# Attention with memory and a spectral filter on one core: a unit's scores split over two score steps, PSUM divided 3+2+3, and a new written-out order

## The chip, the core and the metric

The kernel runs on one core of a Trainium2 chip. The core has five engines with their own instruction streams: TensorE (PE, matmuls; its weight loads are listed as PEld), VectorE (DVE), ScalarE (ACT), GpSimd (POOL) and SyncE (SP, which here only issues DMAs). PE writes to PSUM, which is divided into eight banks of 512 fp32 columns; ACT and DVE read PSUM and move results to SBUF ("evict" them). The metric is the device time of one execution in microseconds, lower is better; the figure for a kernel is the median of its runs.

## The reference

The input is x, 2048 tokens of 640 features. Three things are computed and mixed: a causal attention in four segments of 512 tokens with 32 heads of 20 features, with a compressed memory carried from segment to segment; a filter in the two-dimensional Fourier domain; and a gate per token. Cut to what matters:

```python
q, k, v = heads(x @ wq), heads(x @ wk), heads(x @ wv)      # 32 heads of 20, 4 segments of 512
for s in range(4):
    p = softmax(qs @ ks.T * 20**-0.5 + causal_mask)
    a_dot = p @ vs
    a_mem = (phi(qs) @ M) / (phi(qs) @ z + 1e-6)           # phi(t) = t+1 if t > 0 else exp(t)
    outs.append(g * a_mem + (1 - g) * a_dot)               # g = sigmoid(beta), per head
    M, z = M + phi(ks).T @ vs, z + phi(ks).sum(0)
a = concat(outs) @ wo
b = irfft2(rfft2(x) * (w_r + 1j * w_i))                    # over tokens and features
gate = sigmoid((x * gate_w).sum(-1, keepdims=True))
return gate * a + (1 - gate) * b
```

## The kernel before

**How the program is made.** The class `Kern` records operations (`Sched.op`, L66): what each reads and writes, which engines can do it (`copy_alts`, L534: ACT or DVE; `either`, L549: DVE or POOL), what it should cost, and which PSUM banks it uses (`Bank`, L32). `Sched.schedule` (L117) takes a long list, `ORDER` (L594), and emits the operations in that order on each engine: an entry is twice the number of the record plus the choice of engine. So the order on every engine and the division of work between engines are written out by hand in that list. `schedule` steps through it with assumed costs only to choose physical banks and DMA semaphores, and from data dependences and bank reuse `emit` (L258) makes the semaphore waits. A queue is kept in order: an instruction that waits holds back all behind it on its engine.

**PSUM.** `POOLS` (L587) gives banks 0 to 3 to the scores (`qk`) and banks 4 to 7 to everything else (`gen`).

**Attention.** A segment has eight groups of four heads, taken in four pairs. A pair has five units (`UNITS`, L588): for each of its two groups the first 128 and the next keys' part (kind 0 and kind 1), and one unit of kind 2, that holds the small diagonal rest of both groups. So there are 80 units. `qk_unit` (L1242) writes the scores of a unit: its four heads have 20 features each and lie in four 32-row strips of the PE array, which work at the same time, each head into its own PSUM bank, so that one unit takes all four banks of `qk`. The pieces of a head are in `PIECES` (L589). Then one ACT instruction (two in the last segment for kinds 1 and 2, 92 in all) at L1278 takes the exponential of all four banks to the tile `ex`:

```python
bank = Bank(4, "qk")
for j, kc, p0, q0, o, n in self.PIECES[kind]:
    for hh in range(4): ...
self.one("act", lambda e, d=d, q=q: e.activation(self.ex.ap(*d), self.ps(bank, *q), ACT.Exp, scale=SC), n, [bank], ...)
```

The next unit's scores need the same four banks, and so wait for that instruction. POOL masks `ex` in place (`mask`, L1296, instructions on L1299), and PE multiplies with v (`pv_flipped`, L1193, for segments 0 to 2; `pv_group`, L1304, for segment 3).

**Beside it.** PE also makes the projections (`proj_tile`, L1042; for the first two groups `proj_direct`, L976, whose results `qkp` feed the first scores), v (`v_part`, L1115), the memory (`mem_read_tile`, `mem_update`) and the Fourier transforms as matrix products (`fft`, L1381). All of these use banks of `gen`, which ACT or DVE evict: qu, q, et (phi's exponential, L1087), va (L1130), Ac, Bt, Pt (L1455), Cp, eo and G (L1501), ub, ot. DVE and POOL fold the input rows (`fold`, L906, tiles xsb and xf) before the first transform, and add Pt to Yt (L1460). All this is laid between the units, so that from 13 to 226 us the units run through the whole program.

**The end.** Where the attention of a segment is done, its sums go through DRAM (u_scr, r_scr), and `finish_tile` (L1522) adds the product with wo to the filter's last step in one bank and evicts it to ot, which is stored. The last segment stays on chip (`last_transposes`, L1505; oTl) and uses wo2, loaded by one DMA (L1554) into the place of wk.

**The first DMAs.** SP issues one xsb load (ld_x), the transposing load of x's first 128 features (xT), beta, half of wk (ld_wka), then the two other xT loads. ACT issues ld_wqa. PE multiplies zeros (`warm_up`) until the first data come.

Of the kernel before, what the change touches and what calls it, by code (L numbers as in the profile page):

```python
# [44 lines left out]
class Op:  # L45
    __slots__ = ("id", "alts", "preds", "succs", "prio", "banks", "nbytes", "npred", "eng", "t0", "t1",
                 "stamp", "need_inc", "dyn", "first", "outside", "name", "dma", "key", "xfer", "lock", "mode", "emode", "hold", "width")


class Sched:  # L50
# [6 lines left out]
    FREE, PORT, LATE = 52.0, (85.0, 55.0), 500.0  # L57
# [59 lines left out]
    def schedule(self, pools, order, nsem=56):  # L117
# [32 lines left out]
        two = False  # L150
# [24 lines left out]
        def head(e):  # L175
# [18 lines left out]
            if o.dma:  # L194
                gate = window()
                if gate is not None:
                    t = max(t, gate.t1 + self.HOPS[e]["dma"])
            if e == "dve" and o.lock:
                t = max(t, free["pool"] + (20.0 if two else -self.PORT[0]))
            elif e == "pool":  # L200
                t = max(t, port - self.PORT[1])
            return t

        while len(self.order) < len(order):
# [20 lines left out]
            free[e] = o.t1 = t + occ  # L225
            if e == "dve" and o.lock:
                port = t + occ
            if e == "pool":
                two = o.lock
# [243 lines left out]
class Kern:  # L473
# [38 lines left out]
    def mms(self, items, r, w, prio, name="", extra=0.0, mode=0):  # L512
# [18 lines left out]
        op = self.Sc.op({"pe": (f, cost, self.DRAIN.get(name, 141.0))}, r=r, w=w, prio=prio, name=name, mode=mode)  # L531
        return op
# [10 lines left out]
    def one(self, eng, fn, n, r, w, prio, per=None, fix=None, name="", after=()):  # L543
# [3 lines left out]
        return self.Sc.op({eng: (fn, fix + per * n, late)}, r=r, w=w, prio=prio, name=name, after=after)  # L547
# [9 lines left out]
    def dma(self, dst, src, nbytes, r, w, prio, tr=False, name="", after=(), queue="sp"):  # L557
# [6 lines left out]
        cost, work, width = self.QUEUE[name] if name in self.QUEUE else self.QUEUE[name, nbytes]  # L564
        queues = ("sp", "act") if name in self.EARLY else (queue,)
        return self.Sc.op({e: (f, cost, 0.0) for e in queues}, r=r, w=w, prio=prio, nbytes=nbytes, name=name, after=after,
# [4 lines left out]
        "ld_W": (620.0, 450.0, 16), "ld_beta": (400.0, 120.0, 16), "ld_big": (500.0, 2900.0, 16), "ld_den": (520.0, 150.0, 16),  # L571
        "ld_fcat": (400.0, 350.0, 16), "ld_g": (500.0, 1900.0, 16), "ld_gc": (580.0, 200.0, 16), "ld_gw": (420.0, 600.0, 16),
        "ld_hm": (600.0, 850.0, 16), "ld_r": (570.0, 700.0, 16), "ld_tt": (530.0, 1650.0, 16), "ld_u": (530.0, 600.0, 16),
        "ld_wka": (520.0, 1100.0, 16), "ld_wkb": (450.0, 1500.0, 16), "ld_wqa": (500.0, 1100.0, 16), "ld_wqb": (500.0, 2200.0, 16),
        "ld_wo": (600.0, 700.0, 16), "ld_wo2": (600.0, 3000.0, 16), "ld_wv": (450.0, 3000.0, 16), "ld_x": (450.0, 830.0, 16),
        "oT": (1300.0, 750.0, 16), "pad2": (370.0, 200.0, 10), "pad": (400.0, 1250.0, 10), ("pkT", 131072): (1260.0, 600.0, 16), ("pkT", 262144): (1280.0, 1100.0, 16),
        ("st_qk", 65536): (450.0, 220.0, 16), ("st_qk", 131072): (480.0, 350.0, 16), ("st_qk", 262144): (480.0, 720.0, 16), "st_g": (430.0, 150.0, 4), "st_o": (660.0, 950.0, 8), "st_out": (560.0, 1900.0, 4),
        "st_part": (430.0, 250.0, 16), "st_r": (480.0, 200.0, 16), "st_u": (520.0, 700.0, 16), ("xT", 131072): (1240.0, 1300.0, 16), ("xT", 262144): (1500.0, 1400.0, 16),
        ("xT", 393216): (1400.0, 2600.0, 16), ("xT", 655360): (2950.0, 2100.0, 16)}
# [7 lines left out]
    POOLS = {"qk": [0, 1, 2, 3], "gen": [4, 5, 6, 7]}  # L587
# [648 lines left out]
    def exo(self, s, g):  # L1236
        return ((s * 8 + g) % self.NEX) * 5120
# [385 lines left out]
```

## Time and profile before

| | us |
|---|---|
| median of 3 runs | 242.91 (242.09 to 248.04) |
| the profiled execution | 240.85 |
| span of its profile, first to last instruction | 238.9 |
| ACT, exponentials of the scores (L1278), busy | 138.7 in 92 instructions |
| POOL, masks (L1299), busy | 122.0 in 224 |
| PE, score matmuls (L529, qkp 20*64), busy | 32.3 in 1280 |
| mean granted PE clock | 0.998 |

Busy time is given per engine. Matmuls overlap, so their rows last longer than the distance from one to the next; the same holds to a smaller degree for ACT and DVE. In the tables of waits "PE psum L529 <- ACT ex L1278" means that a matmul at L529, which writes psum, waited for the exponential at L1278, which writes ex. A line can be a helper's: nearly all matmuls are on L529. In the rows of the timeline the name behind the arrow tells what is read: `psum<-qkp` are scores, `psum<-xT,wq` projections. "xN" counts the instructions merged into a row.

### The profile page before, as it was taken

How to read it: one execution, taken by the hardware profiler on the slowest of the kernel's cores; microseconds unless marked ns; L12 is line 12 of the kernel's file. 1: busy time of each engine (PE TensorE's matmuls, PEld its weight loads, DVE VectorE, ACT ScalarE, POOL GpSimd, SP SyncE). 2: the span in 40 equal slices, each digit the busy share in tenths (PEclk: the TensorE clock that was granted, in tenths of full speed). 3: DMA queues.
4: the chain of work that ended last, by engine and by line, in shares of the span. 5: the costliest groups of instructions: out<-in, count | busy, mean ns of one | idle time of the engine just before them, and what ended most of it. 6: DMA issues, size and time to landing. Idle time of an engine off the chain costs nothing.

```text
span 238.9 us, 10255 instructions
## 1 busy us (share of the span) xinstructions
PE 227.6 (95%) x4361; PEld 140.1 (59%) x4361; DVE 196.6 (82%) x481; ACT 199.5 (83%) x241; POOL 166.7 (70%) x297
## 2 busy tenths in 40 slices
PE   7899999999999999999989999999999999899994
PEld 2575566775456566555646655455645466567794
DVE  0579998889899996898999798997988896846563
ACT  2189688898899999999999979999899988797730
POOL 8523268457969956937974999875889868678730
PEclk9999999999999999999999999999999999999999
DMA  7999849996996876483779572364766995872223
GB/s 171 277 366 233 231 125 185 264 207 149 250 227 158 153 210 178 110 241 72 237 213 261 171 226 62 103 157 144 204 205 162 244 215 83 121 107 83 59 86 111
DMA packets 58928, 42.17 MB, mean 177 GB/s; under 512 B 30020, under 2 KB 55172, under 8 KB 58884
## 3 DMA queue, kind: packets, MB, share of 16 engines
q1 hardware_dynamic: 57844, 40.96, 69.9%
q8 instruction: 34, 0.56, 1.0%
q10 hardware_dynamic: 1040, 0.57, 0.8%
q14 instruction: 10, 0.08, 0.2%
HBM read 23.32 MB, written 12.30 MB: 149 GB/s over the span
## 4 chain that ended last, share of the span: by engine, by line
PE 54%; DVE 19%; ACT 14%; DMA 7%; issue 3%; SPq 1%; DVEq 0%
PE psum L529 48%; ACT ex L1278 9%; PE psum L527 6%; DVE Pt L1455 3%; DMA r_scr<-rc 3%; ACT et L1087 2%; DMA xT<-in_A_x_dram 2%; DMA Wt<-in_B_w_i_dram 2%; DVE xsb L921 2%; DVE xf L916 2%; DVE G L1501 1%; DVE va L1130 1%; DVE q L540 1%; DMA r<-r_scr 1%; DVE oU L1542 1%
## 5 line engine op out<-in xcount | busy, mean ns | idle before, releaser
L1278 ACT ACTIVATE ex<-psum 128x2048 bf16<-128x2048 f32 (+4 forms) x92 | 138.7, 1508 | 12.2 <-PE psum L529 10.1
L1299 POOL TENSOR_SCALAR_AFFINE_SELECT ex<-ex 128x256 bf16<-128x256 bf16 (+2 forms) x224 | 122.0, 567 | 37.2 <-ACT ex L1278 33.7
L529 PE MATMUL psum<-qkp 20*64 20x64 bf16 (+5 forms) x1280 | 32.3, 270 | 2.2 <-ACT ex L1278 2.0
L529 PE MATMUL psum<-xT,wk 128*128 128x256 bf16 (+1 forms) x280 | 33.9, 273 | 0.2
L529 PE MATMUL psum<-xT,wq 128*128 128x512 bf16 (+1 forms) x135 | 30.7, 380 | 0.8 <-DMA xT<-in_A_x_dram 0.8
L529 PE MATMUL psum<-wv,xT 128*32 128x321 bf16 (+3 forms) x400 | 30.0, 301 | 0.3 <-DVE va L1130 0.3
L1455 DVE TENSOR_TENSOR Pt<-psum,Wt 128x642 bf16<-128x642 f32 x32 | 25.6, 822 | 2.2 <-PE psum L529 1.9
L529 PEld LDWEIGHTS psum<-qkp 20*64 20x64 bf16 x1280 | 13.3, 102 | 19.7 <-ACT ex L1278 15.4
L529 PEld LDWEIGHTS psum<-xT,wk 128*128 128x128 bf16 (+1 forms) x280 | 19.9, 97 | 6.5 <-DMA wk<-in_A_wk_dram 0.6
L527 PE MATMUL psum<-wo,oU 128*32 128x320 bf16 x480 | 21.9, 300 | 0.7 <-DVE oU L1550 0.5
L921 POOL TENSOR_TENSOR xsb<-xf 128x320 bf16<-128x320 bf16 (+2 forms) x12 | 9.5, 790 | 16.1 <-DVE xsb L921 12.4
L529 PEld LDWEIGHTS psum<-wv,xT 128*32 128x32 bf16 (+1 forms) x400 | 14.6, 96 | 7.5 <-issue 2.6
L1130 DVE TENSOR_TENSOR va<-psum,ebx 128x320 bf16<-128x320 f32 x32 | 15.2, 484 | 4.4 <-ACT gate L1128 2.1
L529 PE MATMUL psum<-big,Ac 128*128 128x160 bf16 (+2 forms) x96 | 18.1, 258 | 0.4 <-DVE Pt L1455 0.3
L529 PE MATMUL psum<-big,Cp 128*128 128x321 bf16 (+1 forms) x96 | 18.0, 302 | 0.2 <-DVE G L1501 0.2
L529 PE MATMUL psum<-ex,va 128*32 128x64 bf16 (+3 forms) x576 | 17.4, 257 | 0.4 <-DVE mem L1175 0.2
L1501 DVE TENSOR_TENSOR G<-eo,psum 128x320 bf16<-128x320 f32 x32 | 14.7, 483 | 3.6 <-PE psum L529 2.6
L540 DVE CAST ot<-psum 128x320 bf16<-128x320 f32 x21 | 10.1, 491 | 9.1 <-PE psum L527 5.9
L529 PE MATMUL psum<-tt,Yt 128*128 128x256 bf16 (+1 forms) x96 | 16.5, 276 | 0.5 <-DVE Yt L1460 0.2
L529 PEld LDWEIGHTS psum<-ex,va 128*32 128x32 bf16 x576 | 10.8, 96 | 9.6 <-POOL ex L1299 1.3
L1087 ACT ACTIVATE et<-qu 128x512 bf16<-128x512 bf16 x25 | 15.6, 631 | 0.2
L527 PEld LDWEIGHTS psum<-wo,oU 128*32 128x32 bf16 x480 | 11.9, 96 | 5.4 <-issue 1.4
(99 smaller groups left out, 392.7 us busy)
## 6 DMA issues: line engine op xcount, KB each, us to landing
qkp<-qk_scr SPq DMA_DIRECT2D x28, 160.0 KB
tt<-tab_tt SPq DMA_DIRECT2D x8, 512.0 KB, 4.5
qk_scr<-qu SPq DMA_DIRECT2D x12, 256.0 KB, 3.1
u_scr<-ub SPq DMA_DIRECT2D x12, 256.0 KB, 3.7
xsb<-in_A_x_dram SPq DMA_DIRECT2D x8, 320.0 KB, 6.5
oU<-u_scr SPq DMA_DIRECT2D x15, 128.0 KB, 2.9
out_dram<-ot SPq DMA_DIRECT2D x12, 160.0 KB
Wt<-in_B_w_r_dram SPq DMA_DIRECT2D x16, 80.2 KB, 2.6
```

Source lines behind the costliest of these rows:

```text
L527: h = e.matmul(dst, wt, r_, start=st, stop=sp_, **{**kw, "tile_position": (0, q), "skip_group_check": True})
L529: h = e.matmul(o_, l_, r_, start=st, stop=sp_, **kw)
L540: alts["dve"] = (lambda e: e.tensor_copy(dst(), src()), 67 + 1.04 * n, 68.0)
L916: self.either(lambda e, r=r, op=op: e.tensor_tensor(xf.ap(r * 642, [321, 2], [1, 320]), xs.ap(o, [D, 2], [1, 320]), xs.ap(o + 320, [D, 2], ...
L921: self.either(lambda e, dst=dst, src=src, d0=d0, n=n, op=op: e.tensor_tensor(xs.ap(o + dst, [D, 2], [1, n]), xf.ap(src + d0, [321, 2], [1, ...
L1087: self.one("act", lambda e: e.activation(et.ap(0, [1, L]), qsl(), ACT.Exp), L, [qb], [b("et", pi_)], late, fix=95, name="phi_exp")
L1130: self.one("dve", lambda e: e.tensor_tensor(va.ap(i * H * VW + h0 * VW, [VW, nh], [1, DH]), self.ps(bank, 0, [DH, nh], [1, DH]), self.ebx. ...
L1278: self.one("act", lambda e, d=d, q=q: e.activation(self.ex.ap(*d), self.ps(bank, *q), ACT.Exp, scale=SC), n, [bank], [self.exb(s, 2 * pr + ...
L1299: self.one("pool", lambda e: e.affine_select(self.ex.ap(e0 + d0, [1280, 4], [1, n], np_=np_), self.ex.ap(e0 + s0, [1280, 4], [1, n], np_=np_),
L1455: self.one("dve", lambda e, ri=ri, Pt=Pt, Wt=Wt, wo_=wo_, bank=bank: e.tensor_tensor(Pt.ap(ri * 322, [644, 2], [1, KD]), self.ps(bank, 0, ...
L1501: self.one("dve", lambda e, q=q, n2=n2, bank=bank, eo=eo: e.tensor_tensor(self.G.ap(n2 * D + 639 * q, [1 - 2 * q, 320]), eo.ap(q, [1, 320] ...
L1542: self.either(lambda e, c=c: e.tensor_tensor(oT.ap(c * L, [1, L]), oT.ap(c * L, [1, L]), self.r4[s].ap(0, [1, L]), ALU.mult), L, [b("r4", ...
```

## The change

1. **Scores.** `qk_unit` writes heads 0 to 2 of its unit and head 3 of the following unit in one step, interleaved piece by piece. The first step of a segment also writes its own head 3, the last step of a segment writes heads 0 to 2 alone.
2. **PSUM.** Three banks for heads 0 to 2, two for head 3 (one written while the other is read), three for everything else.
3. **Exponentials.** Each of the 92 becomes two: one over three heads and one over head 3 (`"y" + name`), with separate dependence keys ("d"). The masks and the product with v depend on both.
4. **The order list** is written anew (2,424 entries instead of 2,328), with other choices of engine for some evictions, folds and additions; SP starts with the three xT loads and ld_wka is on ACT's queue.
5. **wo2** is loaded in five DMAs, one per 128 rows, and each product waits for its own.
6. **The step through the list** in `schedule` assumes other DMA times, instruction fetches of PE, and the DVE/POOL port. One of this reaches the program: a POOL operation of the locked kind (two inputs), or the one after it, gets a dependence on the last locked DVE operation ahead of it (`o.dyn.append(ldv)`). Three small DVE constants are now of the locked kind.

The diff, cut to its core:

```diff
@@ Sched
-    FREE, PORT, LATE = 52.0, (85.0, 55.0), 500.0
+    FREE, PORT, LATE = 52.0, (85.0, 55.0), 0.0
...
             if e == "dve" and o.lock:
                 port = t + occ
+                ldv = o
             if e == "pool":
-                two = o.lock
+                if (o.lock or two) and ldv is not None:
+                    o.dyn.append(ldv)
+                two, ldv = o.lock, None
...
-    POOLS = {"qk": [0, 1, 2, 3], "gen": [4, 5, 6, 7]}
+    POOLS = {"qk": [0, 1, 2], "qy": [3, 4], "gen": [5, 6, 7]}
...
@@ attend
-                self.qk_unit(s, pr, u, parts)
+                k = pr * len(self.UNITS) + u + 1
+                self.qk_unit(s, pr, u, parts, (k // len(self.UNITS), self.UNITS[k % len(self.UNITS)]) if k < 4 * len(self.UNITS) else None)
...
+    def exk(self, s, g, keys):
+
+        return [self.exb(s, g, k + x) for k in keys for x in (("",) if k[0] == "m" else ("", "d"))]
...
-    def qk_unit(self, s, pr, u, unit):
-        self.Sc.group += 1
-        b = self.b
-        prio = self.texp(s, 2 * pr, u)
-        bank = Bank(4, "qk")
+    def qk_part(self, s, pr, unit, heads, bank):
+
+        b = self.b
         gps, kind = unit
         width = 128 if kind == 2 else 512
         items, rb = [], []
...
+        return items, rb, 256 if kind == 2 else 512
+
+    def qk_unit(self, s, pr, u, unit, after):
+        self.Sc.group += 1
+        b = self.b
+        prio = self.texp(s, 2 * pr, u)
+        gps, kind = unit
+        bank, first = Bank(3, "qk"), pr == u == 0
+        parts, banks = [self.qk_part(s, pr, unit, (0, 1, 2), bank)], [bank]
+        if first:
+            self.ahead = Bank(1, "qy")
+            parts.append(self.qk_part(s, pr, unit, (3,), self.ahead))
+            banks.append(self.ahead)
+        bank3 = self.ahead
+        cols = max(p[2] for p in parts)
+        if after is not None:
+            self.ahead = Bank(1, "qy")
+            parts.append(self.qk_part(s, *after, (3,), self.ahead))
+            banks.append(self.ahead)
+            cols = cols + parts[-1][2] if first else max(cols, parts[-1][2])
+        ths = [th for n_ in range(max(len(p[0]) for p in parts)) for p in parts if n_ < len(p[0]) for th in p[0][n_]]
+        self.mms([(th, cols / len(ths)) for th in ths], [x for p in parts for x in p[1]] + banks, [], prio - self.QK_LEAD, name="qk", mode=1)
...
-            self.one("act", lambda e, d=d, q=q: e.activation(self.ex.ap(*d), self.ps(bank, *q), ACT.Exp, scale=SC), n, [bank],
...
+            d3, q3 = (d[0], [d[1][0], 3]) + d[2:], (q[0], [512, 3]) + q[2:]
+            self.one("act", lambda e, d=d3, q=q3: e.activation(self.ex.ap(*d), self.ps(bank, *q), ACT.Exp, scale=SC), 3 * n, [bank],
+                     [self.exb(s, g, k) for g, k in keys], prio - self.QK_LEAD, name=name)
+            d1, q1 = (d[0] + 3 * d[1][0],) + d[2:], (q[0],) + q[2:]
+            self.one("act", lambda e, d=d1, q=q1: e.activation(self.ex.ap(*d), self.ps(bank3, *q), ACT.Exp, scale=SC), n, [bank3],
+                     [self.exb(s, g, k + "d") for g, k in keys], prio - self.QK_LEAD, name="y" + name)
...
-            self.dma(lambda: self.wo2.ap(0, [D, 5], [1, D]), lambda: dap(self.wo_d, 0, [D, P], [P * D, 5], [1, D]), P * 5 * D * 2,
-                     [], [b("wo2")], self.texp(3, 0) + 2.0, name="ld_wo2", after=[b("wka"), b("wkb")])
+            for c in range(5):
+                self.dma(lambda c=c: self.wo2.ap(c * D, [1, D]), lambda c=c: dap(self.wo_d, c * P * D, [D, P], [1, D]), P * D * 2,
+                         [], [b("wo2", c)], self.texp(3, 0) + 2.0, name="ld_wo2", after=[b("wka"), b("wkb")])
```

More of the change, by code (lines that the diff above doesn't have):

```diff
@@ L197, in head @@
                     t = max(t, gate.t1 + self.HOPS[e]["dma"])
+            if e == "pe":
+                n = o.count * (4 if o.mode < 0 and o.emode == 2 else 1)
+                k = (npe + n + 48) // 256
+                if k > 1:
+                    t = max(t, fetched[k] - 15.0 * max(0, k * 256 - 48 - npe))
+            if port_free:
+                return t
             if e == "dve" and o.lock:
@@ L201, in head @@
                 t = max(t, port - self.PORT[1])
+                if o.lock or two:
+                    if ldv is not None:
+                        t = max(t, ldv.t1 + self.HOPS["pool"]["dve"])
+                    elif pos["dve"] < len(queue["dve"]) and queue["dve"][pos["dve"]].lock:
+                        x = head("dve", True)
+                        if x is not None and x <= t - 50.0:
+                            t = max(t, free["pool"] + 21.0)
             return t
@@ L225, in schedule @@
             free[e] = o.t1 = t + occ
+            if e == "pe":
+                npe += o.count * (4 if o.mode < 0 and o.emode == 2 else 1)
+                while nblk < (npe + 48) // 256:
+                    nblk += 1
+                    fetched[nblk + 1] = max(sum(ring) / 16, o.t1 + 1300.0) + 1100.0
             if e == "dve" and o.lock:
                 port = t + occ
+                ldv = o
             if e == "pool":
-                two = o.lock
+                if (o.lock or two) and ldv is not None:
+                    o.dyn.append(ldv)
+                two, ldv = o.lock, None
             if o.dma:
@@ L541, in copy_alts, with one @@
         return alts
-    def one(self, eng, fn, n, r, w, prio, per=None, fix=None, name="", after=()):
+    def one(self, eng, fn, n, r, w, prio, per=None, fix=None, name="", after=(), lock=False):
         fix0, per0, late = {"act": (65, 0.833, 110.0), "dve": (67, 1.04, 68.0), "pool": (132, 0.945, 50.0)}[eng]
@@ L546, in one @@
         fix = fix0 if fix is None else fix
-        return self.Sc.op({eng: (fn, fix + per * n, late)}, r=r, w=w, prio=prio, name=name, after=after)
+        return self.Sc.op({eng: (fn, fix + per * n, late)}, r=r, w=w, prio=prio, name=name, after=after, lock=lock)
     def either(self, fn, n, r, w, prio, name="", after=()):
@@ L563, in f @@
                 return e.dma_start(d_, s_)
-        cost, work, width = self.QUEUE[name] if name in self.QUEUE else self.QUEUE[name, nbytes]
+        cost, work, width, late = self.QUEUE[name] if name in self.QUEUE else self.QUEUE[name, nbytes]
         queues = ("sp", "act") if name in self.EARLY else (queue,)
-        return self.Sc.op({e: (f, cost, 0.0) for e in queues}, r=r, w=w, prio=prio, nbytes=nbytes, name=name, after=after,
+        return self.Sc.op({e: (f, cost, late) for e in queues}, r=r, w=w, prio=prio, nbytes=nbytes, name=name, after=after,
                           dma=True, xfer=work, hold=tr and nbytes > 500000, width=width)
```

62 lines of the change are left out of this document (35 added, 27 removed), and 198 rows, old and new, of the table ORDER.

## The prediction

> **What bounds the kernel now.** First the page: busy shares, then the chain that ended last.
>
> ```profile
> PE 227.6 (95%) x4361; PEld 140.1 (59%) x4361; DVE 196.6 (82%) x481; ACT 199.5 (83%) x241; POOL 166.7 (70%) x297
> PE 54%; DVE 19%; ACT 14%; DMA 7%; issue 3%; SPq 1%; DVEq 0%
> ```
>
> PE is hardly ever idle and carries half the chain. Then the table by stretch (us; busy us of PE, PEld, DVE, ACT, POOL, each with its count; clock; DMA), which shows how close the others run in the middle:
>
> ```profile
> 100.00:120.00 20.00, 19.42 (x325) 11.23 (x324) 18.56 (x46) 19.51 (x24) 14.57 (x30) 1.00 0.63 177
> 140.00:160.00 20.00, 19.07 (x298) 10.20 (x294) 18.45 (x37) 18.80 (x21) 17.95 (x32) 1.00 0.42 115
> ```
>
> ACT is as full as PE there. Third, the timeline of one turn, ACT's rows and then PE's (start us, us):
>
> ```profile
> 163.38 1.88 ACT L1278 ACTIVATE ex<-psum 128x2048 bf16<-128x2048 f32 x1
> 165.15 0.59 ACT L538 ACTIVATE Cp<-psum 128x512 bf16<-128x512 f32 x1
> 165.75 1.03 ACT L1278 ACTIVATE ex<-psum 128x1024 bf16<-128x1024 f32 x1
> 166.67 0.59 ACT L538 ACTIVATE qu<-psum 128x512 bf16<-128x512 f32 x1
> 167.33 1.88 ACT L1278 ACTIVATE ex<-psum 128x2048 bf16<-128x2048 f32 x1
> ```
> ```profile
> 165.31 0.32 PE L529 MATMUL psum<-qkp 20*64 20x64 bf16 x24 [0.27 <-ACT ex L1278]
> 166.83 0.42 PE L529 MATMUL psum<-qkp 20*64 20x320 bf16 x16 [0.28 <-ACT ex L1278]
> ```
>
> The scores (qkp) start 0.05 us after an exponential ends (163.38 + 1.88 = 165.26, then 165.31), take 0.3 to 0.4, and the next exponential starts 0.1 later. All four score banks are one unit's, so PE and ACT take turns; ACT fills its turn off with an eviction, PE stands. A full turn is 1.88 + 0.05 + 0.42 + 0.08 = 2.43 us. Fourth, the waits (us in total, times, longest), and the timeline's first loads:
>
> ```profile
> PEld psum L529 <- ACT ex L1278: 15.4, 49, 0.6
> PE psum L529 <- ACT ex L1278: 2.0, 8, 0.3
> ```
> ```profile
> 1.25 1.21 SPq L561 DMA_TRANSPOSE xT<-in_A_x_dram  x1
> 3.60 2.63 SPq L561 DMA_TRANSPOSE xT<-in_A_x_dram  x2
> 7.86 0.40 PE L529 MATMUL psum<-xT,wq 128*32 128x512 bf16 x4 [0.83 <-DMA xT<-in_A_x_dram]
> ```
>
> The 15.4 is idle time of the weight loader, most of it under a matmul that still streams. To see PE's own loss I took the starts of successive groups of matmuls in the timeline, less the columns streamed (the 512-column rows follow each other in 0.215 us, so 0.42 ns a column) and a change of tile shape at about 0.1 us (projection to projection is 0.108 apart at the least, projection to scores 0.201). Lost in all: 16.1 us. Of it 3.0 to 3.5 before scores that wait for an exponential, 6.7 where a group waits for one of the four other banks to be evicted, 1.3 at 5.7 to 7.9 us for the two last xT loads, 4 to 5 for data, instruction issue and small rests.
>
> **The change, part by part.**
> *Scores three and one.* A unit's heads 0 to 2 now go with head 3 of the next unit. Matmuls stay 1,280, but a step lasts as long as its longer part: the diagonal units (24 matmuls, 0.32 us) now run beside a part of 0.43, so 16 x 0.11 = 1.8, and the first step of each segment writes head 3 twice, 512 more columns, 4 x 0.21 = 0.9. Together +2.6 us (2.56 before rounding), on PE's path. Against it, walking PE's queue through both order lists (a number is twice the record's number plus the choice of engine) I count 229 and 215 changes of tile shape: 14 x 0.11 = -1.5.
> The turn: three heads' exponential takes 1.45 us (the rows of 2048 and 1024 elements give 0.171 + 0.000834 x elements), after which its banks are free, and head 3's, whose scores lie ready, covers the 0.05 + 0.42 + 0.08 of the next scores. What PE regains lies between 2.0 (the waits of its matmul rows) and 15.4 (all of the loader's); I take 3.5, the loss counted above, because the rest lies under streaming matmuls. What is late next is ACT.
> *Exponentials in two parts.* 92 more instructions. A 2048 row is followed after 1.77 (163.38 to 165.15), not 1.88, so 0.11 of each overlaps the next; two parts occupy 1.34 + 0.49 = 1.83. So +0.06 each, 92 x 0.06 = 5.5 us of ACT. The order list moves evictions: ACT loses 4 of Ac, 2 each of Bt, Cp, oTl and the first qkp, and gains 3 of ub, 2 of ot, 1 of qu, at their rows less 0.11: -2.9. Net +2.6. ACT is idle 19.9 of the 213 us from 13 to 226 (sum of the table's stretches); that covers it: 0, bounds 0 and +2.6.
> The Trainium skill (ScalarE: Activation LUTs, What ACT_TABLE_LOAD costs) gives 186 ns plus 0.833 per element, successive ones overlapping by about 93. That would make the split 92 x 0.093 = 8.6 us, an estimate from that page; the trace's overlap here is 0.11, and the sum goes by the trace.
> *PSUM 3+2+3.* The general pool falls from four banks to three. I followed its 326 uses from first matmul to the end of the eviction: 797.6 us held, 432 filling, 127 waiting for the evicting engine, 238 in eviction; three to four held at any time. Three banks offer 3 x 238.9 = 717, less than is held now. The list answers that: fills interrupted by other work go from 168 to 126, those with scores inside from 64 to 30, and the columns and shape changes between a bank's first and last matmul from 374 to 273 us, so about 797.6 - 100 = 697 stay. With 0.06 us from release to reuse and use only from 6 to 235 us (3 x 229 = 687), 30 bank-us are missing, or 10 us of PE. A quarter off the 127 (the longest thing that an eviction waits behind on ACT falls from 1.77 to 1.34) closes it: 32. Bounds: -2.2 (a third off the 6.7) and +10; I take +1.5, nearer the rows that close it.
> *Start.* SP now issues the three xT loads first and wk goes to ACT's queue behind wq: the last two start at 0.78 + 1.21 = 1.99 instead of 3.60, 1.6 earlier. The first xsb load is pushed behind them by 1.21 + 2.63 = 3.8, and with it POOL's and DVE's first folds (at 5.72 and 7.69); the chain from 18 to 35 us is DVE's, though DVE is idle in most of the first 11. Beta too comes later on SP; it feeds constants that the first v evictions want near 20 us. Bounds -1.6 and +1; I take -1.2.
> *The rest of the order.* POOL gains 6 additions of Yt (0.73 against DVE's 0.39), 2 of oU, a gate table and small ones, less 2 folds: about +7.6 us in 72 of idleness, DVE +0.9 in 42. POOL's two-input operations now wait for the last such DVE operation before them; masks queue behind, and the last masks gate the product with v. POOL waits 33.7 us for exponentials, which hides it: 0, bounds -1 and +1. Of data and issue waits I take back 0.7 of some 4.5 (bounds 0 and 2).
> *Last weights.* wo2 in five loads instead of one: four more issues of 0.6, 2.4 us of SP, which waits 21.3 us for PE in all; the oT loads and output stores behind them could come late if that cover went, by up to 2.4. They sit between loads due some 20 us before use: 0.
>
> Sum: +2.6 - 1.5 - 3.5 + 1.5 - 1.2 - 0.7 = -2.8. The profiled execution took 240.85 (span 238.9), so 238.05 on its terms. It ran 2.06 under the median of the three runs, 242.91; on that footing the forecast is 240.1.
>
> **The rivals.**
> 1. *Evictions get quicker too, faster.* With shorter exponentials the bank waits fall by a third, -2.2 instead of +1.5: 240.1 - 3.7 = 236.4. For it: 127 us of waiting for the evicting engine; fewer interrupted fills. Against: a bank less.
> 2. *Three banks are too few, slower.* If the eviction waits stay as they are, the 10 us come in full: 240.1 + 8.5 = 248.6, worst from 60 to 200 us, where 3.3 to 3.6 of four banks are held. It decides once holds stay over about 690 us in all. Against: the shorter exponentials.
> The Trainium skill (TensorEngine Tiling (Array Packing), PSUM Bottleneck) says that packing speeds up TensorE but not PSUM's evacuation. This speaks for the second rival; the 6.7 us against 3.5 above agree that evictions cost more than scores do.
> 3. *ACT becomes the bound, no gain.* From 100 to 120 us ACT is idle for 0.5. If the turn was only as long as ACT's work, the 3.5 are not regained and up to the 2.6 are added: 243.6 to 246.2, about 244.5. Against: ACT's idle 19.9 us elsewhere.
>
> **How the numbers follow.** Forecast 0.43 (own range 238 to 242), rival 1 0.27, rival 3 0.17, rival 2 0.13. The range 235 to 246.5 takes in rivals 1 and 3 and leaves out most of the second. By more than 2%, about what can be told from no change here, means under 238.05 or over 247.8: faster is 0.8 of rival 1 and a fifth of the forecast, 0.31; slower is 0.7 of rival 2 and a sixth of rival 3, 0.12; the rest 0.57.
>
> **What would show it.** Right: scores start while a 512-element exponential runs, and waits of PE and its loader for ex shrink to a third; the first full run of projection matmuls starts at about 6.3; general banks are held 690 us or less. Wrong: longer PE waits for ub, Bt, Cp, Pt, va (second rival), or ACT without gaps and PE's unchanged (third). A DVE chain that still ends near 35 us would make the start worthless.

## The result, and the profile after

The changed kernel takes 252.91 us (median of 4 runs, 250.94 to 254.12) against 242.5 for the kernel before in the same session: ratio 1.0437, 95% interval 1.0336 to 1.0538. It is slower by over 2%, outside the forecast's range of 235 to 246.5. Its profiled execution took 252.1 us, with a span of 250.4 (before: 240.85 and 238.9). The comparisons leave disturbed runs out; one kernel below has no ratio because too few of its runs were left.

The page of the kernel after: busy shares, two of the rows by 40 slices (6.26 us each), and the chain that ended last.

```profile
PE 233.4 (93%) x4361; PEld 142.7 (57%) x4361; DVE 204.6 (82%) x474; ACT 202.5 (81%) x327; POOL 172.4 (69%) x310
...
PE   7989999999976999999999998999989989899994
...
PEclk9999999999996799999999999999999999889999
...
PE 53%; DVE 24%; DMA 9%; SPq 5%; ACT 3%; issue 3%; POOL 2%; DVEq 0%
```

ACT's share of the chain fell from 14% to 3%, which is what the new scores were to do, but DVE's rose from 19% to 24%. The row PEclk shows what no row of before showed at that place: near 78 us and near 217 us TensorE was granted less than its full clock.

**Where the time went.** I put the start of each of the 80 score steps of the two traces side by side. Step 16 begins at 70.4 us (before 70.8), step 20 at 85.1 (80.0), step 24 at 97.9 (90.8), step 72 at 214.7 (206.3), step 76 at 228.3 (216.4). So the loss grows most at two places: by 7.5 us between steps 16 and 24, and by 3.5 between steps 72 and 76. (The new order also moves other work between the steps, so these are not yet the price of the two places; a run below with the same order gives that.) Counted as in the prediction (starts of successive groups less columns and shape changes), TensorE loses 26.4 us instead of 16.1: waits for a general bank 14.8 instead of 6.8, waits for score banks 0.9 instead of 3.5, the rest 10.7 instead of 5.8. Columns and shape changes add 1.1. That makes 8.0 - 2.6 + 4.9 + 1.1 = 11.4 of the 11.5 us of span.

The first place, in the table by stretch (us; busy us of PE, PEld, DVE, ACT, POOL; granted clock; DMA), a row of the kernel before and then three of the kernel after:

```profile
74.00:78.00 4.00, 4.00 (x85) 2.54 (x83) 3.83 (x14) 3.83 (x6) 3.82 (x7) 1.00 0.60 163
```
```profile
70.00:74.00 4.00, 3.17 (x71) 1.71 (x68) 3.98 (x6) 4.00 (x7) 2.92 (x7) 1.00 0.76 136
74.00:78.00 4.00, 1.01 (x10) 0.70 (x11) 4.00 (x7) 1.70 (x3) 4.00 (x8) 0.89 0.03 5
78.00:84.00 6.00, 6.00 (x61) 3.58 (x61) 4.69 (x12) 3.15 (x4) 2.77 (x6) 0.50 0.69 176
```

From 74 to 78 PE works for 1.01 of 4.00 us, while DVE and POOL are both full; then PE is busy all the time at half the clock. The timeline of DVE there, in the kernel after (start us, us):

```profile
72.03 0.42 DVE L1130 TENSOR_TENSOR phq<-phq,et 128x512 bf16<-128x512 bf16 x1
...
72.59 1.56 DVE L1130 TENSOR_TENSOR phk<-phk,et 128x512 bf16<-128x512 bf16 x1
...
74.16 0.30 DVE L1438 TENSOR_TENSOR Macc<-Macc,psum 128x154 f32<-128x154 f32 x1
...
74.54 2.99 DVE L1130 TENSOR_TENSOR phk<-phk,et 128x512 bf16<-128x512 bf16 x1
77.45 0.48 DVE L1202 TENSOR_TENSOR mem<-psum,dn 128x320 bf16<-128x320 f32 x1
```

and POOL's in the same stretch:

```profile
72.56 1.28 POOL L1363 TENSOR_SCALAR_AFFINE_SELECT ex<-ex 64x512 bf16<-64x512 bf16 x2 [0.94 <-ACT ex L1339]
73.81 0.39 POOL L1046 TENSOR_TENSOR omh<-gg,omh 128x8 bf16<-128x8 f32 x1
74.17 1.70 POOL L1363 TENSOR_SCALAR_AFFINE_SELECT ex<-ex 128x512 bf16<-128x512 bf16 x3
75.84 1.41 POOL L1524 TENSOR_TENSOR Yt<-Pt 128x321 bf16<-128x321 bf16 x2
77.20 1.06 POOL L1363 TENSOR_SCALAR_AFFINE_SELECT ex<-ex 128x256 bf16<-128x256 bf16 x2
```

The same minimum of two SBUF tiles (L1130) takes 0.42, then 1.56, then 2.99 us. Less their own 0.42 the two long ones got in near 73.7 and 77.1, where one of POOL's instructions gives way to the next (73.81 and 77.20). In the kernel before, POOL has a row of nine masks without a gap at nearly the same time, and a minimum that starts inside it takes 0.41 us; after that one no operation on two SBUF tiles stands on VectorE until 80.06:

```profile
70.27 5.20 POOL L1299 TENSOR_SCALAR_AFFINE_SELECT ex<-ex 128x256 bf16<-128x256 bf16 x9 [2.13 <-ACT ex L1278]
```
```profile
70.88 0.41 DVE L1100 TENSOR_TENSOR phk<-phk,et 128x512 bf16<-128x512 bf16 x1
```

In the kernel after, two evictions stand behind the long minima on DVE's queue (Macc at 74.16, mem at 77.45), and PE waits for exactly their banks (a bracket gives the idle time alone; counted as above, the two stops are 1.32 and 2.63 us):

```profile
74.51 0.39 PE L551 MATMUL psum<-xT,wk 128*128 128x256 bf16 x2 [1.25 <-DVE Macc L1438]
...
77.98 0.31 PE L551 MATMUL psum<-big,Ac 128*128 128x161 bf16 x1 [2.47 <-DVE mem L1202]
```

The same happens twice more, shortly before and inside the second place: a normalization (oU times r, at 196.86 us) takes 1.98, a product that makes a gated table (fbg, at 213.19) takes 2.44, PE stops for 1.10 and 1.42 us, and the clock is halved again for 3.4 us. DVE, POOL and PE at the later one:

```profile
213.19 2.44 DVE L1067 TENSOR_TENSOR fbg<-fcat,gbc 128x512 bf16<-128x512 bf16 x1
215.56 1.00 DVE L1565 TENSOR_TENSOR G<-eo,psum 128x320 bf16<-128x320 f32 x2
```
```profile
210.84 2.88 POOL L1363 TENSOR_SCALAR_AFFINE_SELECT ex<-ex 128x256 bf16<-128x256 bf16 x5
213.70 1.39 POOL L1614 TENSOR_TENSOR oU<-oU,mT 128x640 bf16<-128x640 bf16 x1
```
```profile
216.61 0.32 PE L551 MATMUL psum<-G,fbg 128*32 128x320 bf16 x4 [1.24 <-DVE G L1565]
```

The 10.2 us at half clock cost up to 5.1.

The Trainium skill (SBUF — State Buffer, Who interferes with whom) says that a DVE instruction with two SBUF inputs contends with a GpSimd instruction that reads SBUF, that the shared port pair is an exclusive lock, and that issue order decides who is blocked. The trace agrees as far as that goes (the mask at 72.56 began 34 ns before the minimum's 72.59). But in the kernel before no such operation was over 0.58 us longer than its shortest, about one mask (0.48 to 0.70); here the one at 74.54 was kept out for 2.59 us, over five POOL instructions that followed each other without a gap.

### The profile page after: what moved, and what is told of

Same layout as the page of the kernel before. It is cut to its first block, busy times and chain, and to the rows that moved or that the text cites. A ratio compares the mean times of both kernels' runs of the same rounds, so it can differ in the third digit from the quotient of the medians.

```text
span 250.4 us, 10376 instructions
## 1 busy us (share of the span) xinstructions
PE 233.4 (93%) x4361; PEld 142.7 (57%) x4361; DVE 204.6 (82%) x474; ACT 202.5 (81%) x327; POOL 172.4 (69%) x310
## 4 chain that ended last, share of the span: by engine, by line
PE 53%; DVE 24%; DMA 9%; SPq 5%; ACT 3%; issue 3%; POOL 2%; DVEq 0%
PE psum L551 47%; PE psum L549 6%; DMA wv<-in_A_wv_dram 4%; DMA tt<-tab_tt 4%; SPq L584 3%; DVE G L1565 3%; DVE phk L1130 2%; DVE Pt L1519 2%; ACT ex L1339 2%; SPq L586 2%; DVE oU L1606 2%; DMA qk_scr<-qu 1%; DVE Ac L563 1%; DVE xsb L951 1%; POOL ex L1363 1%
## 5 line engine op out<-in xcount | busy, mean ns | idle before, releaser
L1339 ACT ACTIVATE ex<-psum 128x1536 bf16<-128x1536 f32 (+4 forms) x92 | 108.0, 1174 | 11.3 <-PE psum L551 10.5
L1342 ACT ACTIVATE ex<-psum 128x512 bf16<-128x512 f32 (+4 forms) x92 | 46.2, 507 | 2.3 <-PE psum L551 2.0
L551 PE MATMUL psum<-qkp 20*64 20x64 bf16 (+5 forms) x1280 | 35.6, 273 | 0.8 <-ACT ex L1339 0.5
L551 PE MATMUL psum<-xT,wk 128*128 128x256 bf16 (+1 forms) x280 | 31.6, 275 | 1.3 <-DVE Macc L1438 1.3
L551 PE MATMUL psum<-wv,xT 128*32 128x321 bf16 (+3 forms) x400 | 29.4, 301 | 1.6 <-DMA wv<-in_A_wv_dram 1.0
L551 PEld LDWEIGHTS psum<-qkp 20*64 20x64 bf16 x1280 | 14.9, 104 | 18.0 <-ACT ex L1339 5.6
L1524 POOL TENSOR_TENSOR Yt<-Pt 128x321 bf16<-128x321 bf16 x22 | 15.9, 729 | 9.6 <-DVE phq L1129 4.3
L951 POOL TENSOR_TENSOR xsb<-xf 128x320 bf16<-128x320 bf16 (+2 forms) x11 | 8.1, 743 | 19.9 <-DVE xsb L951 10.0
L551 PE MATMUL psum<-big,Ac 128*128 128x161 bf16 (+2 forms) x96 | 16.3, 265 | 2.6 <-DVE mem L1202 2.5
L563 DVE CAST ot<-psum 128x320 bf16<-128x320 f32 x19 | 9.1, 486 | 9.0 <-PE psum L549 6.6
```

Source lines behind the costliest of these rows:

```text
L551: h = e.matmul(o_, l_, r_, start=st, stop=sp_, **kw)
L563: alts["dve"] = (lambda e: e.tensor_copy(dst(), src()), 67 + 1.04 * n, 68.0)
L951: self.either(lambda e, dst=dst, src=src, d0=d0, n=n, op=op: e.tensor_tensor(xs.ap(o + dst, [D, 2], [1, n]), xf.ap(src + d0, [321, 2], [1, ...
L1339: self.one("act", lambda e, d=d3, q=q3: e.activation(self.ex.ap(*d), self.ps(bank, *q), ACT.Exp, scale=SC), 3 * n, [bank], [self.exb(s, g, ...
L1342: self.one("act", lambda e, d=d1, q=q1: e.activation(self.ex.ap(*d), self.ps(bank3, *q), ACT.Exp, scale=SC), n, [bank3], [self.exb(s, g, k ...
L1524: fn = lambda e, r=r, a0=a0, a1=a1, op=op, Pt=Pt, Yt=Yt: e.tensor_tensor(Yt.ap(r * 322, [1, KD]), Pt.ap(a0 * 322, [1, KD]), Pt.ap(a1 * 322 ...
```

## The experiments

The theories at first: T1, VectorE is locked out by POOL because the added waits of POOL bunch its masks; T2, three general banks are too few; T3, the new order is itself late. Four kernels took the parts apart.

**Without the added waits.** From the kernel after:

```diff
-                if (o.lock or two) and ldv is not None:
-                    o.dyn.append(ldv)
```

> The changed kernel without the added dependence of POOL's two-input operations on the last such DVE operation; order, banks and scores stay. Theory 1 (the added waits hold POOL back, the masks behind them pile up, and the pile then keeps DVE's two-input operations out for up to 3 us, PE stops and its clock falls): most of the 10 us comes back, 242 to 246, POOL's waits for DVE fall by over 10 us. Theory 2 (three general banks are too few): 250 to 253. Theory 3 (the new order in itself is late): 250 to 253, with the stalls at the same places near 74 and 216 us.

Measured: 249.2 us, ratio 1.0243 (1.0174 to 1.0313). None of the three expectations covers that. In the profiled run, the longest of the four (250.61 us), the first place is unchanged (stops of 1.32 and 2.63 us, then 6.8 us at half clock); the second is milder, with no fall of the clock at 217 us. The shortest (246.68) had a mean granted clock of 1.000. By the medians the waits account for about 2 of the 4.4%; the long lock-outs of the first place are there without them.

**Only the added waits**, in the kernel before (the same two lines, with `ldv` kept as in the diff):

> The kernel before with nothing but the added dependence of POOL's two-input operations, and of the operation behind one, on the last locked DVE operation ahead in the list. Theory 1: slower by 4 to 9 us, 246 to 251, with POOL idle behind DVE. Theories 2 and 3: no change, within 1%.

Measured: 243.28 us, ratio 1.0023 (0.9993 to 1.0052). In the old order they cost nothing that can be told, which T1 had priced at 4 to 9 us.

**Only the new order**, in the kernel before: four score banks and four general ones, whole exponentials, no added waits; its list is the list of after with the parts that don't exist left out.

> The old scores, exponentials and banks (4+4), no added waits, but every queue in the new order, head 3's exponentials left out of the list and the last weights in one load. Theory 1: within 2% of the kernel before, 240 to 246. Theory 2: the same, for there are four general banks. Theory 3: 249 or more.

Measured: 252.98 us, ratio 1.0422 (1.0371 to 1.0472). The time is that of the kernel after, though there are four general banks; but TensorE's 29.4 us of stops are made up otherwise (14.0 for score banks, 4.4 for general ones), since the order was laid for the other scores. T3's 249 or more came true, and not the 240 to 246 of the other two. But this kernel loses its time at other waits than the kernel after, so it shows only that the fourth bank doesn't cure this order.

**Exponentials and last weights split**, in the old order:

> The kernel before in its own order with four score banks, but each exponential in two parts, heads 0 to 2 and then head 3 of the same unit, directly behind each other, and the last weights in five loads. Theories 1, 2 and 3: the split costs 0.06 us each, 5.5 us of ACT; as the turn between scores and exponential is as long as before plus 0.06, between 0 and +5, I expect +2 to +4 (244.5 to 246.5). If the split itself were the cause of the loss: 250 or more.

Measured: 247.91 us, ratio 1.0246 (1.0197 to 1.0296). It follows the kernel before to within 0.8 to 2.6 us until 198 us; then scores wait 1.80 us for the load of a padded tile (qkp, their input), and the clock is halved for 10.2 us. That is above the 244.5 to 246.5 expected and under the 250 that would have made the split the cause.

**Letting VectorE go first.** Of T1 the lock-out stands and the added waits as its cause fall. The trace gave a sharper theory, T1': it matters only that masks, which wait for nothing on VectorE, run without a gap while an operation that shares the port with them, and evictions behind it, stand on VectorE. The kernel after with two waits at the first place (numbers are those of the operations):

```diff
+        for x, y in ((378, 1066), (359, 1076)):
+            ops[x].preds.append(ops[y])
         for o in ops:
             o.dyn, o.t1 = [], None
```

> The kernel after, with two waits more on POOL: the first mask of the row that begins at 72.56 us there waits for the minimum ahead of it in the list (which began 34 ns behind it and took 1.56 us instead of 0.49), and the second mask of that row waits for the next minimum (which took 2.99 us). Nothing else changes. T1' (masks that run without a gap keep VectorE's two minima out, the evictions queued behind them come late, TensorE stops for 1.32 and 2.63 us and then runs at half the clock for 6.8 us): both minima take under 0.8 us, the two stops are under 0.5 us each, the clock does not fall near 78 us, score step 24 starts near 91 to 92 us instead of 97.9, and 243 to 248 us against 252.9. T2 (three general banks are too few there, whatever VectorE does): the stops move to other evictions, step 24 still after 96 us, 250 us or more. T3 (the new order is late all along): step 24 earlier, but half of it is lost again by the end, 249 or more.

Measured: 247.11 us, ratio 1.0156 (1.0081 to 1.0231). Its timeline of DVE, then of POOL, and its table by stretch:

```profile
73.92 0.42 DVE L1132 TENSOR_TENSOR phk<-phk,et 128x512 bf16<-128x512 bf16 x1
...
74.34 0.31 DVE L1440 TENSOR_TENSOR Macc<-Macc,psum 128x154 f32<-128x154 f32 x1
...
74.72 0.62 DVE L1132 TENSOR_TENSOR phk<-phk,et 128x512 bf16<-128x512 bf16 x1
75.27 0.48 DVE L1204 TENSOR_TENSOR mem<-psum,dn 128x320 bf16<-128x320 f32 x1
```
```profile
74.41 0.66 POOL L1365 TENSOR_SCALAR_AFFINE_SELECT ex<-ex 64x512 bf16<-64x512 bf16 x1 [1.47 <-DVE phk L1132]
75.42 0.66 POOL L1365 TENSOR_SCALAR_AFFINE_SELECT ex<-ex 64x512 bf16<-64x512 bf16 x1 [0.34 <-DVE phk L1132]
```
```profile
74.00:78.00 4.00, 3.85 (x81) 2.08 (x72) 3.93 (x14) 3.60 (x6) 3.25 (x7) 1.00 0.52 111
78.00:84.00 6.00, 4.97 (x85) 3.12 (x84) 5.22 (x15) 5.92 (x11) 5.93 (x11) 1.00 0.91 221
```

The minima take 0.42 and 0.62, PE works 3.85 of 4.00 us in the stretch where it had worked 1.01, and the clock stays full. POOL waits 1.47 and 0.34 us for it, and no stop of TensorE takes the place of the two. Step 24 begins at 94.4 us, 3.5 earlier than in the kernel after, but not at the 91 to 92 expected; step 16 was already 1.0 late against the kernel before. T2 would have kept the kernel at 250 us or more; it did not. Near 212 us a stop of 1.4 us for an eviction and 3.4 us at half clock are still there.

**The second place too**, with three more pairs: (1917, 2134), (1924, 2142), (1996, 2105).

> The same two waits, and three more of the same kind near the end: two masks at 196.9 us wait for the two normalizations ahead of them in the list (the first took 1.99 us), and one mask at 213.3 us waits for the gating of the table (2.44 us instead of about 0.8). T1': the two late stops of TensorE (1.10 and 1.42 us) and the half clock from 217 us for 3.4 us go too: 3 to 5 us less than with the first two waits alone, 240 to 244.5 us, so not slower than before by more than 1%. T2 and T3: within 1.5 us of the run with the first two waits alone.

Measured: 245.51 us, ratio 1.0111 (1.0049 to 1.0174); span 243.8, clock 0.999, no stretch at half clock before the end. That is 1.6 us less than with two waits, not the 3 to 5 that T1' gave, and by the intervals the two runs can't be told apart: what the later three waits bring is shown by the trace alone, in which the lock-outs and the half clock near 213 us are gone. The kernel after has the same order, so its steps can be set against these: it is 0.3 us ahead at step 16, 5.3 behind at step 24, 5.7 at step 72, 6.5 at step 76 and 6.6 at the end. So the first place costs some 5.6 us and the second 0.9. Waits for a general bank, counted in the same way, fall from 14.8 to about 10 us, against 6.8 with four banks: T2 falls as the cause of the main part, and whether the last 3 to 4 us of waits come from the missing bank or from the order was not separated. Five waits on an engine that is idle 30% of the time took the ratio from 1.0437 to 1.0111.

**A rule in place of the list**, in the kernel after, ahead of the same lines:

```diff
+        l = None
+        for v in order:
+            o = ops[v // 2]
+            if o.eng == "dve" and o.lock:
+                l = o
+            elif o.eng == "pool" and l is not None:
+                o.preds.append(l)
+                l = None
```

> The same as a rule in place of a list: every POOL operation, masks too, waits for the last operation of VectorE that shares the port with POOL and stands ahead of it in the list since the POOL operation before. T1': as good as the hand-picked waits, 240 to 246 us, with VectorE's total excess on such operations under 8 us instead of 14.2. Rival (POOL held at every such place makes its masks late, and the weight loads that wait for ex with them, which is what cost time in the run without the added waits turned round): 248 us or more, with waits of the loader for POOL ex of more than 3 us in total.

Measured: 245.01 us, ratio 1.0086 (1.005 to 1.0122): as good as the picked waits. VectorE's excess on such operations (their time over the shortest of their kind) falls from 14.2 to 9.0 us (not under 8), none of it over 0.54 at once. The same rule in the kernel before, which has no lock-out of that length:

> The kernel before with the general rule: every POOL operation waits for the last port-sharing operation of VectorE ahead of it in the list since the POOL operation before. T1' (lock-outs are what the rule cures, and before has none longer than one mask): no gain, within 0.8% of before, 241 to 245 us. Rival (the 11.5 us by which VectorE's port-sharing operations are longer than their shortest also cost time in the kernel before): 237 to 240.5 us, faster than both kernels.

Measured: 242.45 us, ratio 1.0001 (0.9974 to 1.0029): the excess falls from 11.5 to 6.6 us and the time stays. There, delays of about one mask cost nothing that can be told; the long ones of the kernel after did.

**Three general banks in the old order** (`"gen": [4, 5, 6]`, the order mended where three don't suffice):

> The kernel before with three general banks of PSUM instead of four, the fourth left unused, and its order mended at the places where three do not suffice (an entry that can't be placed is put behind those that free a bank). T2 (three banks are too few): slower than before by 2 to 4%, 247 to 252 us, with TensorE's waits for a general bank grown from 6.8 to 14 us or more. T1' (the three banks matter only where VectorE is late): within 1.5% of before, 241 to 246 us. My prediction's own term for this was +1.5 us, with -2.2 and +10 as bounds.

Measured: 321.97 us, ratio 1.3256 (1.3173 to 1.3339). A third slower, far outside both expectations: this order, laid for four banks, was not mended by moving single entries. It bounds nothing for the new order, where the run with five waits is the better witness.

**The two splits apart**, in the old order. First the exponentials alone:

> The kernel before in its own order with each of the 92 exponentials in two parts, three heads and then the fourth, back to back on ScalarE; the scores and the banks stay as they were and the last weights stay in one load. My prediction took this split at nothing (2.6 us of ScalarE, hidden by its idle time). If that holds: within 0.6% of before, 241 to 244 us, and the stop of 1.80 us near 204 us that the run with both splits had is gone (it came from the loads in five parts). Rival (ScalarE has no room: what the split adds comes out behind it): 245 to 247 us, with TensorE's waits for the banks of the scores above 8 us in total, and the stop near 204 us is still there.

Measured: 243.92 us, ratio 1.007 (1.0033 to 1.0107), and no stop near 204 us: a little above the 0.6% and under the rival's 245. The loader's waits for an exponential grew, from the 15.4 us of before:

```profile
PEld psum L549 <- ACT ex L1336: 18.5, 52, 0.9
```

TensorE's own waits for score banks are 6.2 us instead of 3.5: ScalarE is busy for 204.8 us instead of 199.5, close to the 5.5 that I had worked out, and what was to hide it did so only in part. Then the last weights alone:

```diff
-            self.dma(lambda: self.wo2.ap(0, [D, 5], [1, D]), ...
+            for c in range(5):
+                self.dma(lambda c=c: self.wo2.ap(c * D, [1, D]), ...
```

> The kernel before with its last weights in five loads of 160 KB, all issued where the one of 800 KB stood; nothing else changes. Prediction's term: nothing, so 242 to 243.5 us (within 0.5%). Rival (four issues more on SP's queue make the last loads of the padded tiles late): a stop of TensorE of over 1 us near 204 us and 244.5 us or more.

Measured: 245.11 us, ratio 1.0134 (1.0064 to 1.0205). Its queue of SP and its PE:

```profile
187.24 3.42 SPq L563 DMA_DIRECT2D wo<-in_A_wo_dram  x5
191.08 0.32 SPq L563 DMA_DIRECT2D qkp<-qk_scr  x1
197.72 0.50 SPq L563 DMA_DIRECT2D qkp<-qk_scr  x1
```
```profile
203.09 0.43 PE L529 MATMUL psum<-qkp 20*64 20x512 bf16 x12 [2.17 <-DMA qkp<-qk_scr]
```

The last padded tile's load goes out at 197.72; in the kernel before it went out at 194.07, and its scores ran at 200.19 without a stop. It goes 3.65 us later: the queue was 0.6 late already at 187.24, and five issues take 3.42 us where one took 0.60. PE stops for 2.2 us and then runs 6.8 us at half clock, as the rival said.

**What remains of the loss.** In the run with five waits 4.9 us of span are left. I took single stops of it for the rest (T-rest) and moved what they waited for. A load of a table of the transforms (tt) 5 us earlier, and the last weights' five loads all where the first stands:

> The kernel after with the five hand-picked waits (245.51 us measured), and two moves of loads: the fifth to last table load from its place at 143.6 us to just behind the one that frees its buffer, some 5 us earlier, and the five loads of the last weights all where the first one stands, so that none runs at 201 to 210 us. T-rest (what is left of the loss, 4.9 us of span, sits in a few separate stops: 0.96 us at 149.5 us behind the table, 0.80 and 1.18 us at 211.0 and 216.4 us in which TensorE waited for nothing that the profile shows, while transfers filled the DMA engines): the stop behind the table goes, the two late ones shrink to under 0.4 us if transfers were their cause, 242.5 to 244 us, within 0.5% of before. Rival (the late stops have nothing to do with the loads): the stops stay and 244.5 to 246 us.

Measured: 251.8 us, ratio 1.036 (1.0292 to 1.0427). The loads of u came late in their place, a normalization on VectorE with them, and PE stopped for 1.83 us at 197.8 and ran 6.8 us at half clock. T-rest's time falls here. The late stop for nothing that the profile shows stayed (1.61 us idle up to 219.46), though the loads of the last weights had been moved away from it. Then one move at a time, and both:

> The kernel after with the five hand-picked waits (245.51 us measured, 1.0111 of before) and the last weights in one load of 800 KB where the first of the five stands. If the four issues more on SP's queue are what the split costs (five loads at one place made the kernel before 1.3% slower): no stop of TensorE over 1.2 us at 195 to 220 us, and 243 to 245.5 us. Rival (the bytes early are what does harm, in one load as in five): a stop of over 1.5 us near 198 us again, and 248 us or more. Rival 2 (the last weights don't matter in the new order): within 0.4% of 245.5.

Measured: 246.9 us (244.37 to 250.78), span 243.6 (no ratio). No stop over 1.2 us from 195 to 220, but one of 1.76 us at 81.5 behind another table load. Up to some 100 us after that stop every queue has the same order as in the run with five waits, so the move did not make it.

> The kernel after with the five hand-picked waits, and only the fifth to last table load moved, from its place at 143.6 us to some 5 us earlier. T-rest (the stop of 0.96 us at 149.5 us is that load's alone): the stop goes, score steps from 52 on begin 0.5 to 1 us earlier than with the five waits alone (159.4 there), 244 to 245.5 us. Rival (what is behind the load on the queue comes late in its place): step 52 at 159.4 or later, 245.5 or more.

Measured: 247.1 us, ratio 1.0199 (1.0126 to 1.0271). The stop at the table is gone, and another took its place, 2.08 us at 146.8 us for an eviction (the waits of its PE):

```profile
PE psum L553 <- DVE ub L565: 1.9, 1, 1.9
```

> Both moves together with the five waits. If what remains of the loss is a handful of single stops: 242.5 to 245 us, within 1% of before. Rival (each change of the order brings another evictor late elsewhere, by chance of some tenths of a us): 245 us or more, with at least one stop of over 1 us at a place that neither the run with the five waits nor the other two have.

Measured: 248.25 us, ratio 1.022 (1.0125 to 1.0314). For the table's load the rival holds: in all three kernels that move it (a_free3, a_tt, a_onett) TensorE stands idle for 0.9 to 1.9 us at 143 to 147 us until an eviction to ub ends, and the run with five waits alone has no such stop. For the last weights alone no gain and no harm can be told. The last 1.1% could not be pinned to a part. In the trace with five waits it holds the 1.1 us of columns and shape changes that the prediction counted and 3 to 4 us more of waits for general banks, less some 2 us that the scores no longer wait.

## Why the prediction was wrong

The failed step is the one on POOL in the rest of the order: "POOL's two-input operations now wait for the last such DVE operation before them; masks queue behind, and the last masks gate the product with v. POOL waits 33.7 us for exponentials, which hides it: 0, bounds -1 and +1." I asked what a late mask does to the product with v, and it did nothing. I did not ask what a row of masks does to VectorE, though the row for those masks and the one for the minima stood in the profile. The runs show that this is the main term: 6.6 us of span between the kernel after and the one with five waits (250.4 - 243.8), 7.4 by the medians (252.91 - 245.51), where the term's bounds were -1 and +1. The added waits are not the main part (about 2%, and nothing in the old order): the lock-out of 2.59 us stands in the new order without them, and none in the old order with them is over 1.1 us, so the long ones come with the new places of masks and minima.

Step by step:
- *Scores three and one.* Right: +2.6 - 1.5 = 1.1 predicted for columns and shapes, 1.1 found. Of the 3.5 us of waits for score banks, 2.6 came back. The waits for exponentials did not shrink to the third that was named: the loader's fell from 15.4 to 9.5 us (5.6 and 3.9 for the two parts), TensorE's own from 2.0 to 0.5. The mechanism shows in the trace of after, where the scores begin under the 512-element exponential, in the rows of ACT and of PE:

```profile
99.79 0.59 ACT L1342 ACTIVATE ex<-psum 128x512 bf16<-128x512 f32 x1
...
100.80 1.45 ACT L1339 ACTIVATE ex<-psum 128x1536 bf16<-128x1536 f32 x1
...
103.14 1.45 ACT L1339 ACTIVATE ex<-psum 128x1536 bf16<-128x1536 f32 x1
```
```profile
100.07 0.42 PE L551 MATMUL psum<-qkp 20*64 20x512 bf16 x13
102.48 0.43 PE L551 MATMUL psum<-qkp 20*64 20x320 bf16 x15
```

  From one long exponential to the next it is 2.34 us, and 16 steps in the middle (28 to 44) take 36.6 us instead of 37.7: a gain of 3%, and no more, because ScalarE is full there (48.5 of 50 us busy from 90 to 140), as the third rival said. With the lock-outs cured by five waits it is 36.6 as well.
- *Exponentials in two parts.* Taken at 0, bounds 0 and +2.6: in the old order it costs 0.7%, 1.7 us. ScalarE's idle time was not all where the split lay.
- *PSUM.* The general banks are held 630.8 us instead of my 697, so even less than the 690 that I named as the point of decision. The second rival's rows did appear (PE waits for banks), and its sum was of the right size, but that was luck: its condition (holds over 690) was not met, and with the lock-outs cured the same three banks wait about 10 us instead of 14.8. What is left is 3 to 4 us more than with four banks, against the +1.5 taken. A bank wait says first who is late, not that banks are few.
- *Start.* Worth nothing, as the prediction said it would be if the DVE chain still ended near 35 us. The first full projection run begins at 5.68 us and the first scores at 9.45 instead of 12.8:

```profile
5.68 0.40 PE L551 MATMUL psum<-xT,wq 128*32 128x512 bf16 x4
...
9.45 0.65 PE L551 MATMUL psum<-qkp 20*64 20x512 bf16 x16
...
18.38 0.31 PE L551 MATMUL psum<-wv,xT 128*128 128x320 bf16 x1 [1.02 <-DMA wv<-in_A_wv_dram]
```

  but TensorE then waits 1.02 us for wv, and step 4 begins at 32.1 us in both kernels. Term -1.2, found 0.
- *Last weights.* Taken at 0 with the cover named ("loads due some 20 us before use"). That was true of the loads next to it and not of the padded tile's, whose scores ran 6.1 us after its issue. Found in the old order: +1.3%. In the new order the parts are spread, and putting them back in one load gained nothing that can be told.
- *The clock.* The sum had no term for it. A stop of PE of 1.4 us or more was followed in several traces by 3.4, 6.8 or 10.2 us at half clock, which can cost half that time on top of the stop: up to 3.4 us behind the stop of 2.2 us in the kernel with the last weights split.

## What to carry to other kernels

When an order is laid anew, look at each operation of VectorE with two SBUF inputs and ask whether a row of POOL instructions can start just ahead of it, and which evictions stand behind it on VectorE's queue; here one wait on the less loaded engine at each such place was the cure, and POOL had the slack for it. A DMA issue inserted on a full queue is priced at the tightest load behind it, not at the nearest. And a stop of TensorE of over 1.4 us is to be counted with the half clock that may follow.

## What the runs showed of the hardware

- An operation of VectorE that shares the port with POOL can be kept out for several POOL instructions in a row (2.59 us over five, 1.17 and 1.58 us at two other times in the same trace). At most places it got in at the next boundary of POOL, though those rows had no gap either (26 of the 31 that were held up by over 0.08 us in the trace of after). What decides was not tried and stays open; with POOL waiting the minima took 0.42 and 0.62 us.
- The granted clock fell to 0.50 at stops of TensorE of 1.42 us (for 3.4 us), 1.83, 2.24 and 2.63 us (6.8 us) and 1.80 us (10.2 us), and not at stops of 1.18, 1.82, 2.08 and 2.2 us in other runs. The Trainium skill (TensorE: Matmul & The Clock Gate, Part 1) puts the fall after an idle window of about 3.4 us and says that the window runs free of the kernel. The lengths of 3.4, 6.8 and 10.2 us agree with such a window, and so does the lack of a sharp limit; the measured stops are shorter than one window, and there the measurement decides.
- In six of the ten kernels with the new order TensorE stands idle for 0.9 to 1.7 us near 211 to 219 us for nothing that the profile shows. In the run with five waits:

```profile
216.41 1.38 PE L551 MATMUL psum<-wo,oU 128*32 128x320 bf16 x33 [1.01 <-issue]
```

  In the kernel before the longest such wait of the loader is 0.4 us. The cause stays open.
